# Attention and two feed-forward layers on one core: output halves issued by ScalarE, rests of the third chunk's output weights on GpSimd

## The chip, the core and the metric

The kernel runs on one core of a Trainium2 chip. Its engines each work through a queue of their own in order: TensorE (PE in the rows; PEld is its weight load), VectorE (DVE), ScalarE (ACT), GpSimd (POOL) and SyncE (SP), which here does nothing but issue DMAs. They wait for each other through semaphores. The metric is the time of one execution on the device in microseconds; the time given for a kernel is the median of its runs.

## What is computed

```python
# q, k, v: 4 batches, 8 heads, 576 rows, 64 wide; all float32
scores = scale * np.matmul(q, k.transpose(0, 1, 3, 2))
kth = np.partition(scores, -top_k, axis=-1)[..., -top_k:-top_k + 1]      # top_k = 32
scores = np.where(scores >= kth, scores, -1000000000.0)
scores = scores - np.max(scores, axis=-1, keepdims=True)
attn = np.exp(scores)
attn = attn / (np.sum(attn, axis=-1, keepdims=True) + 1e-09)
x = np.matmul(attn, v)                     # then 2304 tokens x 512
g = x @ w_gate                             # 512 -> 1536
x = (g * (1.0 / (1.0 + np.exp(-g))) * (x @ w_val)) @ w_out    # 1536 -> 512
h = x @ w_in                               # 512 -> 2048
out = (h * np.cos(h)) @ w_out2             # 2048 -> 512
```

## The kernel before

The 2304 tokens are 18 tiles of 128, taken in ten chunks (SIZES: two chunks of one tile, then eight of two). A unit is one tile and one head; there are 144. For each unit TensorE makes the scores (L598, in the first three chunks L591), ScalarE copies them to SBUF (L603), and VectorE finds the 32 largest by four rounds of max (L628) and three of striking out what was found (L631). GpSimd makes two bounds from them (L642, L646), ScalarE masks and exponentiates (L659, L670), TensorE transposes (L692), ScalarE copies (L698), TensorE multiplies by v (L745, L748), ScalarE copies that (rx, L759) and GpSimd scales it (L818, L829). VectorE has a reciprocal per group (L775) that waits for GpSimd (L777).

The first feed-forward layer runs chunk by chunk beside the attention of the chunks behind it: gate and value (L903), copies out of PSUM by ScalarE (L869, L870, L881), products by GpSimd (L957 to L959), the split of the result into a high part (ScalarE, L965) and a rest (GpSimd, L969), and the product with the output weights (L1070). From the third chunk on (c = 2, called PLAIN) float32 factors are split into a part that TensorE multiplies at full rate and a rest; each product is three such products. The second layer (L1407, L1684) follows when all chunks are through.

The output weights come in twelve tiles. For the third chunk, `wo_proc` loads a tile in float32 (L378), ScalarE makes its high part (L386), a subtraction makes the rest in place (L387), and the pair is stored (L390), so that later chunks load it ready-made (L380). Two buffers hold tiles, and a buffer comes free when TensorE has used it and the store has landed. Chunks 0 and 1 load plain weights (L376).

`y_proc` finishes a tile of the first layer's output in two halves: ScalarE copies a half out of PSUM (L1105), TensorE turns it (L1111), ScalarE copies the turned half to SBUF (L1116), and a DMA stores it (L1117) to a buffer in DRAM that the second layer loads. There is one SBUF buffer for halves, so the next half's first copy waits for the store to land. 18 tiles make 36 stores.

The order of each engine's queue is made by a planner when the program is built: every step yields an engine, a cost in microseconds, a function that emits instructions, and a due time; the planner advances a model of the engines and takes, of the steps that are ready on an engine, the one due first. A changed engine or cost of one step therefore shifts the order of everything behind it. A DMA that is emitted inside a step of another engine (as the store at L1117 inside a step of ScalarE that costs 0.27) has no cost in the model, and it stands in the queue of the engine that issues it, behind what was emitted before it. All DMAs share eight semaphores in turn, so a DMA can also have to wait for an earlier one with the same semaphore.

Of the kernel before, what the change touches and what calls it, by code (L numbers as in the profile page):

```python
# [165 lines left out]
def topk_attention_moe_moe(ctx: ExitStack, tc: tile.TileContext, qT, kT, vP, w1, wo1, w2, out):  # L166
    nc = tc.nc
# [4 lines left out]
    y1 = dram.tile([128, KT, NTOK], F32, name="y1")  # L172
# [80 lines left out]
    W1X, W1, WO = {}, {}, {}  # L253
# [52 lines left out]
    def wo_turn(c, f):  # L306
        return ev_wol.setdefault(c * NF1 + f, Event())
# [4 lines left out]
    def wo_index(c, f):  # L312
        return c * NF1 + f
# [51 lines left out]
    def wo_proc(c, f):  # L365
        k = c * NF1 + f
        yield wo_whole[f] if c <= PLAIN else wo_stored[f]
        yield r_wo.gate(wo_index(c, f))
        yield wo_turn(c, f - 1)
        due = moe_due(c, f)  # L370

        def load():
            w = moe.tile([128, 2, DM], F32R if c >= PLAIN else F32, tag="wo", name="wo", bufs=r_wo.n)
            WO[k] = w if c >= PLAIN else w[:, 0]
            if c < PLAIN:
                nc.sync.dma_start(WO[k], wo32[f])  # L376
            elif c == PLAIN:
                nc.sync.dma_start(WO[k][:, 1].bitcast(F32), wo32[f])  # L378
            else:
                nc.sync.dma_start(WO[k].bitcast(F32), wo[f])  # L380

        t = yield "DMA", 1.1 if c <= PLAIN else 1.6, load, due, True
        wo_turn(c, f).set(t - plan.LAT["DMA"], plan)
        if c == PLAIN:
            x = WO[k][:, 1].bitcast(F32)
            yield "ACT", 0.52, lambda: nc.scalar.activation(WO[k][:, 0], x, AF.Copy), due, True  # L386
            t = yield "DVE", 0.75, lambda: nc.vector.tensor_sub(WO[k][:, 1], x, WO[k][:, 0]), due, True  # L387
        ev_wo[c, f].set(t, plan)
        if c == PLAIN:
            t = yield "DMA", 2.1, lambda: nc.sync.dma_start(wo[f], WO[k].bitcast(F32)), due, True  # L390
            wo_stored[f].set(t, plan)
            r_wo.free(wo_index(c, f), t, plan)
# [461 lines left out]
    def moe_due(c, f):  # L854
        return due_unit((FIRST[c] + SIZES[c]) * H) + 20.0 + f * SIZES[c] * H * PACE / NF1
# [236 lines left out]
    def y_proc(c, i):  # L1092
        due = moe_due(c, NF1) - 80.0 * (c >= NCH - 2)
        bank = yt[i % NYB]
        y4 = bank.rearrange("p (f n) -> p f n", f=KT)
        for half in range(2):
            ko = yo_count[0]
            yo_count[0] += 1
            yield r_yo.gate(ko)
            y2 = y4[:, 2 * half:2 * half + 2]  # L1100
            st = {}

            def fetch(y2=y2):
                st["y"] = moe.tile([128, 2, 128], F32, tag="yo", name="yo", bufs=r_yo.n)
                nc.scalar.activation(st["y"], y2, AF.Copy)  # L1105

            yield "ACT", 0.27, fetch, due, True

            def turn(y2=y2):
                for j in range(2):  # L1110
                    nc.tensor.transpose(y2[:, j], st["y"][:, j], ident)  # L1111

            yield "PE", 0.22, turn, due + 2.0, True

            def store(y2=y2, half=half):
                nc.scalar.activation(st["y"], y2, AF.Copy)  # L1116
                nc.sync.dma_start(y1[:, 2 * half:2 * half + 2, i * 128:i * 128 + 128], st["y"])  # L1117

            end = yield "ACT", 0.27, store, due, True
            r_yo.free(ko, end + 2.5, plan)  # L1120
        r_y[i % NYB].free(i // NYB, end, plan)
        ev_y1[i].set(end + 2.5, plan)
# [600 lines left out]
    for c in range(NCH):  # L1723
        for f in range(NF1):
            if c:
                plan.start(wo_proc(c, f))
            if not TURNED[c]:
                plan.start(gemm_proc(c, f))
            elif f % 2:
                plan.start(turned_gemm_proc(c, f // 2))  # L1730
        plan.start(wout_proc(c))
# [52 lines left out]
```

## Time and profile before

| | |
|---|---|
| three runs, median | 1227.88 us (1226.94 to 1229.16) |
| the profiled execution | 1223.17 us |
| its span, first to last instruction | 1221.4 us |
| mean granted TensorE clock | 0.993 |
| TensorE, weight loads | 1169.9 us (96%), 1018.3 us (83%) |
| VectorE | 1002.2 us (82%) |
| ScalarE | 937.9 us (77%) |
| GpSimd | 574.8 us (47%) |
| DMA | 199.96 MB, mean 164 GB/s |

Busy shares of the whole span mix two stages: the attention with the first layer beside it, up to some 756 us, in which VectorE searches, and the rest, in which it hardly does. The rows of the section below are cut by stretch for that reason. A matmul's record reaches over the start of the next one, so a busy TensorE is not by itself one at full rate.

### The profile page before, as it was taken

The page shows a single profiled execution, that of the slowest core. Times are in us where ns is not written, and L with a number is a line of the kernel's source. Part 1 is how long each engine was busy: PE and PEld are TensorE (multiplying, and loading weights), DVE is VectorE, ACT ScalarE, POOL GpSimd, SP SyncE. Part 2 cuts the span into 40 slices and gives each one's busy share as a digit, 9 for nine tenths or more (in the row PEclk, how much of TensorE's full clock was granted, in tenths as well). Part 3 has the DMA queues.
Part 4 walks back from the last instruction along what each step waited for, and adds up shares of the span by engine and source line. Part 5 has one row for each costly group of instructions (what it writes and reads, how often), then busy time and mean ns, then how long its engine had stood idle before and what let it go on. Part 6 is the DMA issues. An engine that isn't in the chain of part 4 may idle for free. (4 is left out here: it accounts for less than half of the span.)

```text
span 1221.4 us, 23299 instructions
## 1 busy us (share of the span) xinstructions
PE 1169.9 (96%) x7720; PEld 1018.3 (83%) x7720; DVE 1002.2 (82%) x1984; ACT 937.9 (77%) x2085; POOL 574.8 (47%) x1036
## 2 busy tenths in 40 slices
PE   5799979999999999999999999999999999999998
PEld 3577646898888898898988898999999998888887
DVE  7999999999999999999999997277867778644541
ACT  4789999898889989898988887446756678755651
POOL 4898976876687876777766765300000000000000
PEclk9799999999999999999999999999999999999999
DMA  7455556665545653656545533463344276443430
GB/s 260 152 189 169 178 159 195 205 205 184 191 152 165 226 176 123 210 181 202 179 150 187 175 121 102 158 215 124 124 166 136 110 249 199 147 122 104 129 104 27
DMA packets 138985, 199.96 MB, mean 164 GB/s; under 512 B 19312, under 2 KB 88432, under 8 KB 138864
## 3 DMA queue, kind: packets, MB, share of 16 engines
q1 hardware_dynamic: 138704, 198.40, 51.1%
q8 instruction: 61, 1.00, 0.3%
q14 instruction: 60, 0.49, 0.1%
q10 hardware_dynamic: 160, 0.07, 0.0%
HBM read 152.28 MB, written 46.14 MB: 162 GB/s over the span
## 5 line engine op out<-in xcount | busy, mean ns | idle before, releaser
L628 DVE MAX8 m<-w 128x8 f32<-128x576 f32 x432 | 309.5, 747 | 1.8
L903 PE MATMUL gv<-x,w 128*128 128x256 f32 x2016 | 271.2, 286 | 0.3 <-ACT hg L870 0.3
L903 PEld LDWEIGHTS gv<-x,w 128*128 128x128 f32 x2016 | 252.2, 191 | 2.9 <-ACT hg L870 0.9
L631 DVE MATCH_REPLACE8 w<-m,w 128x576 f32<-128x576 f32 x288 | 213.0, 742 | 0.0
L1684 PE MATMUL b<-w2o,gp 128*128 128x512 f32 x864 | 202.1, 396 | 0.0
L1684 PEld LDWEIGHTS b<-w2o,gp 128*128 128x128 f32 x864 | 162.4, 188 | 38.7
L1407 PE MATMUL b<-xc,w 128*128 128x288 f32 x1344 | 182.1, 297 | 2.2 <-DVE h L1472 2.2
L1407 PEld LDWEIGHTS b<-xc,w 128*128 128x128 f32 x1344 | 180.2, 189 | 3.3 <-DVE h L1472 2.7
L1070 PE MATMUL y<-wo,gh 128*128 128x512 f32 x400 | 147.1, 414 | 4.1 <-DMA wo<-wo 1.9
L659 ACT ACTIVATE e<-s,b 128x576 f32<-128x576 f32 x144 | 113.5, 789 | 9.8 <-POOL b L642 9.5
L628 DVE MAX8 m<-s 128x8 f32<-128x576 f32 x144 | 107.2, 745 | 12.8 <-ACT s L603 11.6
L670 ACT ACTIVATE e<-e,b 128x576 f32<-128x576 f32 x144 | 114.1, 793 | 4.2 <-POOL b L646 0.3
L603 ACT ACTIVATE s<-sc 128x576 f32<-128x576 f32 x144 | 95.0, 660 | 20.3 <-PE sc L591 16.2
L698 ACT ACTIVATE pt<-tp 128x512 f32<-128x512 f32 (+1 forms) x216 | 101.4, 498 | 11.3 <-PE tp L692 10.7
L631 DVE MATCH_REPLACE8 w<-m,s 128x576 f32<-128x576 f32 x144 | 106.9, 742 | 0.0
L692 PE MATMUL tp<-ident,e 128*128 128x128 f32 x648 | 98.3, 275 | 8.8 <-ACT e L670 3.6
L1070 PEld LDWEIGHTS y<-wo,gh 128*128 128x128 f32 x400 | 75.0, 189 | 26.2 <-issue 4.0
L598 PE MATMUL sc<-K,q 128*128 128x288 f32 (+1 forms) x512 | 92.1, 307 | 3.9 <-ACT s L603 3.6
L692 PEld LDWEIGHTS tp<-ident,e 128*128 128x128 f32 x648 | 77.7, 141 | 19.7 <-ACT pt L698 5.5
L1070 PE MATMUL y<-wo,gl 128*128 128x512 f32 x208 | 84.8, 414 | 3.8 <-POOL wo L249 3.5
L598 PEld LDWEIGHTS sc<-K,q 128*128 128x128 f32 (+1 forms) x512 | 73.4, 183 | 10.8 <-ACT s L603 5.8
L748 PE MATMUL av<-pt,V 128*64 128x256 f32 (+3 forms) x832 | 75.2, 324 | 0.0
(115 smaller groups left out, 2081.6 us busy)
## 6 DMA issues: line engine op xcount, KB each, us to landing
wo<-wo SPq DMA_DIRECT2D x96, 512.0 KB, 3.6
gr<-gd SPq DMA_DIRECT2D x72, 256.0 KB, 3.2
w_raw<-in_w SPq DMA_DIRECT2D x32, 511.8 KB, 4.5
V<-in_vP SPq DMA_DIRECT2D x52, 256.0 KB, 3.0
w<-in_w SPq DMA_DIRECT2D x24, 511.5 KB, 5.7
kx<-in_kT SPq DMA_DIRECT2D x64, 144.0 KB, 3.0
wo<-wo SPq DMA_DIRECT2D x36, 256.0 KB, 3.0
gd<-h SPq DMA_DIRECT2D x32, 288.0 KB, 2.1
```

What stands on the lines that cost most here:

```text
L598: nc.tensor.matmul(sc[:r1, s, :HALF], q[:, a, (t - t0) * 128:(t - t0) * 128 + r1], k[:, s * HALF:s * HALF + HALF], start=a == 0, stop=a == 1)
L603: nc.scalar.activation(st["s"], sc[:, :, :HALF], AF.Copy)
L628: nc.vector.max(out=st["m"][:, 8 * i:8 * i + 8], in_=st["w"] if i else st["s"])
L631: nc.vector.match_replace(out=st["w"], in_to_replace=st["m"][:, 8 * i:8 * i + 8], in_values=st["w"] if i else st["s"], imm_value=LOWEST)
L659: nc.scalar.activation(st["e"], st["s"], AF.Prelu, bias=st["b"][:, 1:2], scale=SCALE, alpha=STEEP)
L670: nc.scalar.activation(st["e"], st["e"], AF.Exp, bias=st["b"][:, 2:3], scale=1.0, accum_out=smT[c, p, g][:, j:j + 1])
L692: nc.tensor.transpose(st["ps"][:, j - j0], e[:, j * 128:j * 128 + 128], ident)
L698: nc.scalar.activation(pt[:, j0:j1], st["ps"][:, :j1 - j0], AF.Copy)
L903: nc.tensor.matmul(gv[g], W1[f, kk // 2][:, a, g, kk % 2], m, start=kk == 0 and i == 0, stop=kk == KT - 1 and i == 2)
L1070: nc.tensor.matmul(bank, m, w, start=f == 0 and n == 0, stop=f == NF1 - 1 and n == len(terms) - 1)
L1407: nc.tensor.matmul(ps[b], w[:, a, side, kk], x[:, e, kk], start=start and kk == 0 and m == 0, stop=kk == 1 and m == 2, skip_group_check=True)
L1684: nc.tensor.matmul(st["o"], g[:, a, cs], W2O[f][:, b], start=f == 0 and i == 0, stop=f == NF2 - 1 and i == 2)
```

## The change

The rest of an output weight tile of the third chunk is made by GpSimd in place of VectorE, with a cost of 1.27 in the planner in place of 0.75. The store of an output half is issued by ScalarE in place of SyncE; the planner's cost of that step stays 0.27.

```diff
         if c == PLAIN:
             x = WO[k][:, 1].bitcast(F32)
             yield "ACT", 0.52, lambda: nc.scalar.activation(WO[k][:, 0], x, AF.Copy), due, True
-            t = yield "DVE", 0.75, lambda: nc.vector.tensor_sub(WO[k][:, 1], x, WO[k][:, 0]), due, True
+            t = yield "POOL", 1.27, lambda: nc.gpsimd.tensor_sub(WO[k][:, 1], x, WO[k][:, 0]), due, True
         ev_wo[c, f].set(t, plan)
...
             def store(y2=y2, half=half):
                 nc.scalar.activation(st["y"], y2, AF.Copy)
-                nc.sync.dma_start(y1[:, 2 * half:2 * half + 2, i * 128:i * 128 + 128], st["y"])
+                nc.scalar.dma_start(y1[:, 2 * half:2 * half + 2, i * 128:i * 128 + 128], st["y"])

             end = yield "ACT", 0.27, store, due, True
```

On ScalarE the first store stands behind its copy as follows; first before, then now, each instruction with the semaphores it waits for (DMAHW are those of DMAs).

```order
L295 ACTIVATE w_7_1765<-w_7_572 128x512 [waits Pool_49]
L1116 ACTIVATE yo<-y_102 128x256 [waits PE_49,Activation_49]
L698 ACTIVATE pt<-tp 128x128 [waits PE_49]
L670 ACTIVATE e,sm<-e,b_1671 128x576
L1049 ACTIVATE gh_1789<-tp 128x256 [waits PE_49]
```

```order
L295 ACTIVATE w_7_1765<-w_7_572 128x512 [waits Pool_49]
L1116 ACTIVATE yo<-y_102 128x256 [waits PE_49,Activation_49]
L1117 DMA y_63<-yo 128x2x128 [waits DMAHW0_49,Activation_49]
L698 ACTIVATE pt<-tp 128x128 [waits PE_49]
L670 ACTIVATE e,sm<-e,b_1671 128x576
L1049 ACTIVATE gh_1789<-tp 128x256 [waits PE_49]
```

The store waits for ScalarE's own semaphore and, in 25 of the 36 cases, for that of an earlier DMA; the copy pt and all behind it now stand behind the store.

On SyncE the same two first stores go, and the loads of the second chunk's output weights (L376) and of keys (kx) move up; one piece of the difference.

```order
 L338 DMA wo_65<-wo 128x512
 L515 DMA qx<-in_qT 64x2x256 x2
-L1117 DMA y_63<-yo 128x2x128
 L376 DMA wo<-wo_65 128x512 x3
-L1117 DMA y_63<-yo 128x2x128
 L490 DMA kx<-in_kT 64x576 x2
 L376 DMA wo<-wo_65 128x512 x3
```

Both stores leave the queue and nothing else moves in these rows.

On GpSimd the first subtraction stands where the third chunk's first layer begins; b are the bounds of a unit, x, th and vv parts of the layer, K a split key. Before:

```order
L818 TENSOR_TENSOR rs<-rx,rs 128x256
L642 TENSOR_TENSOR b_2146<-m,cst 128x2
L646 TENSOR_TENSOR b_2146<-b_2146 128x1
L829 TENSOR_TENSOR x<-rs,x 128x256
L642 TENSOR_TENSOR b_2222<-m,cst 128x2
L501 TENSOR_TENSOR K<-kx,K 64x576
L646 TENSOR_TENSOR b_2222<-b_2222 128x1
L957 TENSOR_SCALAR th<-th 128x256
```

and now:

```order
L818 TENSOR_TENSOR rs<-rx,rs 128x256
L642 TENSOR_TENSOR b_2146<-m,cst 128x2
L387 TENSOR_TENSOR wo<-wo 128x512
L829 TENSOR_TENSOR x<-rs,x 128x256
L646 TENSOR_TENSOR b_2146<-b_2146 128x1
L642 TENSOR_TENSOR b_2218<-m,cst 128x2
L646 TENSOR_TENSOR b_2218<-b_2218 128x1
L501 TENSOR_TENSOR K<-kx,K 64x576
L957 TENSOR_SCALAR th<-th 128x256
```

The subtraction and the product x stand between the two halves of one unit's bounds. From here on all engines' orders differ in small moves up to the end of the attention; the kinds and numbers of matmuls are the same.

## Rows read from the trace of the kernel before

**Rows 1.** Stretches: length, busy us of PE, PEld, DVE, ACT, POOL (instructions).

```profile
0.00:200.00 200.00, 165.35 (x819) 115.05 (x820) 184.72 (x387) 164.70 (x362) 157.94 (x266) 0.96 0.58 185
...
200.00:756.00 556.00, 545.55 (x4155) 491.87 (x4154) 543.88 (x1123) 490.98 (x1192) 402.07 (x745) 1.00 0.55 175
...
204.00:285.00 81.00, 79.77 (x635) 72.18 (x634) 79.92 (x163) 73.29 (x176) 63.66 (x110) 1.00 0.66 212
...
780.00:860.00 80.00, 79.55 (x573) 75.94 (x572) 54.52 (x106) 42.72 (x93) 0.00 (x0) 1.00 0.57 187
...
1020.00:1215.00 195.00, 195.00 (x837) 157.29 (x836) 95.09 (x142) 115.27 (x195) 0.00 (x0) 1.00 0.38 114
```

**Rows 2.** Timeline of PE, one run in each stage: start us, us, what.

```profile
287.85 3.11 PE L903 MATMUL gv<-x,w 128*128 128x256 f32 x24
...
781.57 3.60 PE L903 MATMUL gvl<-x,w 128*128 128x256 f32 x28
```

**Rows 3.** PE's waits, 200 to 780 us: who waits for whom: us, times, longest.

```profile
PE y L1111 <- ACT yo L1105: 2.5, 5, 0.9
PE sc L598 <- ACT s L603: 2.1, 3, 1.3
PE tp L692 <- ACT rx L759: 1.6, 1, 1.6
PE y L1070 <- DMA wo<-wo: 1.2, 2, 0.7
...
PE y L1070 <- POOL gl L969: 0.2, 1, 0.2
```

**Rows 4.** L387 as a group (busy, mean ns); L299 alike: ns least, median, most.

```profile
L387 DVE TENSOR_TENSOR wo<-wo 128x512 fp32r<-128x512 f32 x12 | 10.0, 831 | 0.4 <-ACT wo L386 0.4
...
L299 POOL TENSOR_TENSOR w<-w,w x12: 1265/1276/1288, 113.7 to 186.6; 128x512 fp32r<-128x512 f32 x12
L299 DVE TENSOR_TENSOR w<-w,w x12: 669/690/1523, 115.9 to 188.9; 128x512 fp32r<-128x512 f32 x12
```

**Rows 5.** Timeline of POOL and DVE around one subtraction.

```profile
244.00 0.73 POOL L818 TENSOR_TENSOR rs<-rx,rs 128x256 f32<-128x256 f32 x1
...
244.06 1.22 DVE L387 TENSOR_TENSOR wo<-wo 128x512 fp32r<-128x512 f32 x1
245.20 0.08 DVE L631 MATCH_VALUE_LOAD w<-m,w 128x8 f32 x1
```

**Rows 6.** DVE's waits, 200 to 760 us.

```profile
DVE sm L775 <- POOL sm L777: 3.8, 4, 1.7
DVE m L628 <- ACT s L603: 3.5, 6, 1.3
```

**Rows 7.** Issues of L1117 and of ScalarE's only DMAs: ns least, median, most.

```profile
L1117 SPq DMA_DIRECT2D y<-yo x36: 360/371/663, 166.3 to 853.7; - x36
...
L465 ACTq DMA_DIRECT2D qr<-in_qT x2: 547/627/707, 0.9 to 1.5; - x2
```

**Rows 8.** SyncE's wait at the stores; the stores' size and median us to landing.

```profile
SPq L1117 <- ACT yo L1116: 56.8, 20, 5.5
...
y<-yo SPq DMA_DIRECT2D x36, 128.0 KB, 1.9
```

**Rows 9.** Timeline of SP and PE behind the first store.

```profile
166.75 5.10 SPq L376 DMA_DIRECT2D wo<-wo  x3
...
169.47 2.03 PE L1070 MATMUL y<-wo,xw 128*128 128x512 f32 x2 [2.33 <-DMA wo<-wo]
```

**Rows 10.** Timeline of ACT, SP and PE at the store of 206.69 us.

```profile
206.69 0.38 ACT L1116 ACTIVATE yo<-y 128x256 f32<-128x256 f32 x1
206.95 0.65 ACT L603 ACTIVATE s<-sc 128x576 f32<-128x576 f32 x1
...
207.09 0.37 SPq L1117 DMA_DIRECT2D y<-yo  x1
...
209.80 0.40 ACT L870 ACTIVATE hg<-gv 128x256 f32<-128x256 f32 x1
...
210.25 1.70 PE L903 MATMUL gv<-x,w 128*128 128x256 f32 x12
```

**Rows 11.** Timeline of ACT at the store of 288.44 us; idle before in brackets.

```profile
288.44 0.36 ACT L1116 ACTIVATE yo<-y 128x256 f32<-128x256 f32 x1
...
290.88 0.78 ACT L659 ACTIVATE e<-s,b 128x576 f32<-128x576 f32 x1 [0.66 <-POOL b L642]
```

## The prediction

> **What bounds the kernel now.** I read the table of stretches first. From 200 to 756 us, the bulk of the attention with the first feed-forward layer beside it, VectorE is busy 543.88 of 556.00 us and TensorE 545.55 [rows 1]: both look full. ScalarE has 556.00 - 490.98 = 65.0 us without work, one part in nine, and GpSimd more. After 756 us VectorE is no longer full (54.52 of 80.00 us from 780 to 860) while TensorE is (79.55 of 80.00) [rows 1]. So the question is whether the time from 200 us on is set by VectorE, which this change relieves, or by TensorE, which it doesn't.
>
> A busy TensorE need not be a full one, since a matmul's record reaches over the start of the next. So I compare spacing: 24 matmuls of L903 inside the attention take 3.11 us, and 28 of the same form in the last chunk, after all attention, 3.60 us [rows 2]. Taking off one record's tail of about 0.29 us, that is 2.82/23 = 0.123 and 3.31/27 = 0.123 us from start to start. TensorE does not run any looser beside the attention than where nothing but matmuls is left. What it loses shows in its list of waits: ten groups, 10.2 us together from 200 to 780, nearly all ended by ScalarE, and by GpSimd 0.2 us [rows 3]. My reading: from 200 us to the end TensorE's work sets the time, and an edit counts by what it does to these ten microseconds. VectorE's full row is a second, nearly equal bound.
>
> The Trainium skill (Perfetto Trace Analysis, Identifying the Most-Contended Engine) says that matmul busy time is a poor measure and that the share of weight loading should be used. By it TensorE is 491.87/556.00 = 88% full and VectorE 98%, and relieving VectorE would pay. The trace agrees about the busy row, but the share has no 100% here: between 1020 and 1215 us, where TensorE is busy without a break, weight loading is 157.29/195.00 = 81% [rows 1]. By the rule the sum would be the first rival's below.
>
> **Part 1: rests of the third chunk's output weights, VectorE to GpSimd.** VectorE loses 12 subtractions of 831 ns mean, 10.0 us busy [rows 4]; a record overlaps the next by 0.08 us (the one at 244.06 lasts 1.22, the next row starts at 245.20 [rows 5]), so 12 x 0.75 = 9.0 us of its queue go. If VectorE alone set the time, that is -9.0. With TensorE as the bound only those of its waits can go that hang on the attention's progress: scores waiting for the copy out of PSUM, 2.1 us, and transposes waiting for the copy rx, 1.6 us [rows 3], 3.7 us at most. They end at ScalarE, not at VectorE, and VectorE's own waits are 3.8 us for GpSimd and 3.5 for ScalarE [rows 6], so not all of it can go. Between 0 and -9.0 I take **-2.0**.
>
> GpSimd gains 12 subtractions. It does the same form at L299 in 1.276 us median [rows 4]: 12 x 1.276 = 15.3 us, in the stretch where VectorE now does them (204 to 285 us). GpSimd is busy 63.66 of 81.00 us there [rows 1], so 17.3 us idle hold 15.3, with nothing to spare. Behind each subtraction in its queue stand the bounds of the softmax (L642, L646), the gate products and the rests of gh that TensorE multiplies; in the new order the first one stands between the two halves of one unit's bounds. Each weight tile is ready later too: 1.276 - 0.831 = 0.45 us, plus up to one GpSimd operation ahead of it (0.73 us, L818 [rows 5]). All twelve passed on would be 12 x 1.2 = +14 us; none, 0. TensorE now waits for GpSimd 0.2 us in 580 [rows 3], the planner's cost for the moved step (1.27) is the measured one, and it places the matmuls behind it accordingly. I take **+1.0**, near the low end.
>
> One row speaks for the move: at 244.06 the subtraction on VectorE takes 1.22 us instead of the 0.69 median of its like at L299, while GpSimd's L818 started at 244.00 [rows 4, 5]. The Trainium skill (SBUF — State Buffer, Who interferes with whom) says why: a VectorE instruction with two SBUF inputs contends with a GpSimd instruction that reads SBUF, and the second to issue waits. After the change VectorE has only one-input searches there, and by this rule GpSimd would also get some time back; without it the charge stays at 15.3 us. The sum goes by the rows alone.
>
> **Part 2: 36 stores from SyncE's queue to ScalarE's.** SyncE loses 36 issues of 0.371 us [rows 7] and the waits in front of them, 56.8 us in 20 cases [rows 8]; what stood behind can leave earlier. Most had no reader in a hurry: the wait of TensorE on weight loads is 1.2 us from 200 on [rows 3]. The 2.33 us at 169.47, where the load stands right behind a store at 166.75 [rows 9], lies before 200 us, where TensorE is busy only 165.35 of 200.00 us [rows 1] and the attention decides when the third chunk starts. Bounds 0 and -3.5; I take **-0.5**. The moment of the store itself hardly changes, since SyncE already stands waiting when ScalarE is done (L1116 ends 206.69 + 0.38 = 207.07, issue 207.09 [rows 10]).
>
> ScalarE pays. Its store has to wait for the end of the copy before it (the program makes it wait for ScalarE's own semaphore), and the queue behind it waits for the issue. Today the next operation starts 0.12 us before the copy's end (206.95 against 207.07 [rows 10]). After: 0.03 us to the issue, 0.37 us issue, and the overlap lost, 0.52 us a store; 36 x 0.52 = 18.7 us. The only DMAs that ScalarE issues today took 0.627 us median, another shape [rows 7], which would make it 0.78. The planner still charges 0.27 for copy and store, so it moves nothing out of the way. Two stores lie before 200 us, eight after 780, where ScalarE is busy only 42.72 of 80.00 us [rows 1] and which I cost at nothing (the idle half covers them; uncovered they are 8 x 0.52 = 4.2 us). The 26 between: 13.5 us if all of it reached TensorE, 0 if ScalarE's idle time took it all. I followed each of the 26 in the timeline from the copy to the next idle time that makes up 0.52 us, asking whether TensorE meanwhile started on an output of ScalarE with less than that to spare. In 15 it did. The one at 206.69 is such a case: no idle time before the copy hg at 209.80, which ends at 210.20, and L903 starts at 210.25, so 0.47 us reach it [rows 10]. In 11 not: after 288.44 comes 0.66 us of idle time at 290.88 before anything of TensorE is touched [rows 11]. The 15 shortfalls add to 5.5 us; where two follow closely, the first also gives the second some slack. I take **+4.5**.
>
> A DMA also waits for a semaphore of an earlier DMA in 25 of the 36 stores, which on ScalarE would hold more than the store. I cost it at nothing: SyncE has issued all that stands ahead of such a store and then waits for ScalarE, 56.8/20 = 2.8 us on average, longer than the 1.9 us in which such a store lands [rows 8]. If that cover goes, each of the 25 can hold ScalarE for up to 1.9 us.
>
> **Sum.** -2.0 + 1.0 - 0.5 + 4.5 = +3.0 us. The profiled execution took 1223.17 us (span 1221.4 and 1.8 around it), 0.4% under the median of the three runs, 1227.88. Profiled: 1226.2; as a median: **1230.9**.
>
> **Rivals.** *VectorE sets the time* (faster). It is 98% busy and from 204 to 285 us it has 81.00 - 79.92 = 1.1 us idle [rows 1]; if every matmul run hangs on attention results, the 9.0 us go through, 1218.9, and if half go through and ScalarE's gaps fill, about 1224. Against it stands the equal spacing of matmuls [rows 2]. It decides if TensorE's idle time in 200 to 756 falls well under its present 10.4 us. *The gaps vanish in ScalarE's idle time* (no change): 65 us of idle time take 13.5, VectorE's relief and GpSimd's load cancel, and the end stays near 1228. For it: only 15 of 26 stores meet a tight reader at all. *GpSimd comes late* (slower): 15.3 us into 17.3 us idle delays weights and bounds, TensorE waits 0.8 us at each of 12 tiles, 9.6 us in place of the 1.0: 1227.88 + 3.0 + 8.6 = 1239.5. It decides once the wait for a rest is longer than the matmuls that the planner has put ahead of it. Against: the planner counts the move at its measured price.
>
> **Chances.** Forecast (ScalarE's gaps reach TensorE, +1.5 to +8) 0.40; no change 0.34; VectorE decides 0.17; GpSimd late 0.09. Range 1224 to 1236: it holds the first two and the weaker half of VectorE's case, and leaves out 0.09 below and 0.09 above. Changes under 0.2%, 2.5 us, can't be told from none here. Slower by more: 0.46; within: 0.37; faster: 0.17.
>
> **What would show it.** Right: ScalarE's next operation after L1116 starts about 0.4 us after its end; TensorE's waits ended by ScalarE grow from under 9 us to about 13 between 200 and 780; VectorE has 5 to 10 us idle more in the attention, and its last search ends earlier than 756 by less than 9 us. GpSimd is 75 to 79 us busy from 204 to 285. Wrong: TensorE's idle time shrinks and the end moves by what VectorE saved; or TensorE's waits on GpSimd and weights grow by microseconds; or the stores' wait for a DMA semaphore shows as a ScalarE gap of over a microsecond.

## The result, and the profile after

The changed kernel takes 1242.05 us in the median of six runs (1238.74 to 1246.35), the kernel before 1228.24: a ratio of 1.0111, with an interval of 1.0090 to 1.0131, or 13.6 us (11.1 to 16.1) more. The forecast was +3.0, and its range ended at 1236. Single executions of one kernel lie mostly within 3 us of its median, a few as far as 7. The first profiled execution of the kernel before (1223.17 us) lies 5 us under its median, and that of the changed kernel (1246.35 us) is the slowest of its six, 4.3 us over its own. So the two traces lie 23 us apart where the kernels lie 13.6, and a difference between them is evidence only if it is larger than what a second execution of the kernel before, of 1230.06 us, shows against the first; it is called the second execution of before. In what follows a ratio of 0.1% is 1.23 us.

The stretches of the changed kernel that answer to [rows 1], in the same columns, and one short stretch behind the attention:

```profile
200.00:756.00 556.00, 540.42 (x4073) 482.78 (x4072) 530.98 (x1090) 482.22 (x1170) 407.22 (x746) 1.00 0.55 173
204.00:285.00 81.00, 78.00 (x622) 70.28 (x622) 76.73 (x161) 74.04 (x177) 70.05 (x119) 1.00 0.61 199
780.00:860.00 80.00, 74.20 (x499) 67.84 (x499) 37.37 (x75) 31.28 (x74) 7.26 (x11) 0.96 0.51 160
800.00:810.00 10.00, 8.88 (x53) 8.88 (x54) 2.81 (x7) 3.05 (x9) 0.00 (x0) 0.66 0.29 87
```

VectorE is 12.9 us less busy from 200 to 756 than before and TensorE 5.1, with 82 matmuls fewer in the same time; against the second execution of before (538.46 and 543.01 us, 4109 matmuls) it is 7.5 us, 2.6 us and 36 matmuls. Either way VectorE was relieved and TensorE got less done. The loudest row is the third. From 780 to 860 us TensorE runs 499 matmuls where it ran 573 [rows 1]. That is where the prediction charged nothing. Part of the difference is only lag, since this execution comes to 780 us with some 12 us of work behind; the table further below takes that out.

The waits of TensorE from 200 to 780 us, as in [rows 3], and below them those of VectorE from 200 to 760, as in [rows 6]:

```profile
PE y L1111 <- ACT yo L1105: 4.1, 7, 2.7
PE gv L903 <- ACT hg L870: 3.6, 5, 1.3
PE sc L598 <- ACT s L603: 2.0, 5, 0.7
...
PE y L1070 <- POOL gl L969: 0.3, 1, 0.3
```

```profile
DVE m L628 <- ACT s L603: 12.5, 14, 2.0
DVE sm L775 <- POOL sm L777: 6.9, 6, 2.5
```

ScalarE is what both wait for most. TensorE waits for the copy of an output half (L1105) 4.1 us in place of 2.5 (2.0 in the second execution of before), once 2.7 us long, and VectorE waits for ScalarE's copies 12.5 us in place of 3.5 (6.2 in the second). TensorE waits for GpSimd as little as before.

Why is L1105 late? Two views of the store say it: its issues with the time from issue to landing, and the idle time of ScalarE in front of L1105 (us, times).

```profile
L1117 ACTq DMA_DIRECT2D y<-yo x36: 366/366/417, 167.3 to 874.9; - x36
...
DMA to landing us min/median/max: 1.8/2.7/6.4
```

```profile
  DMA y<-yo: 10.7, 8
```

Before, the store landed in 1.9 us in the median and 3.8 at most, and ScalarE waited 5.2 us in six places for it. Now it is 2.7 in the median and 6.4 at most, and 10.7 us in eight places. That sum alone doesn't tell what a kernel loses: with the stores still on SyncE it is 8.4 us with the rests moved and 10.3 with a planner's number changed, two kernels that come further below. The longest wait, in the timeline of ScalarE (idle time before in brackets):

```profile
793.81 0.38 ACT L1116 ACTIVATE yo<-y 128x256 f32<-128x256 f32 x1 [2.02 <-PE y L1111]
794.22 0.37 ACTq L1117 DMA_DIRECT2D y<-yo  x1
794.63 0.38 ACT L978 ACTIVATE th<-gvl 128x256 f32<-128x256 f32 x1 [0.44 <-ACT yo L1116]
796.11 0.42 ACT L965 ACTIVATE gh<-vv 128x256 fp32r<-128x256 f32 x1 [1.09 <-DVE vv L943]
800.69 0.38 ACT L1105 ACTIVATE yo<-y 128x256 f32<-128x256 f32 x1 [4.16 <-DMA y<-yo]
```

Both costs of the store stand in five rows: the hole of 0.44 us behind the copy (at least that behind all 36 copies), and then 4.16 us in which ScalarE, with one buffer for halves, stands waiting for a store that takes 6.45 us to land. SyncE's timeline at that time, of the changed kernel and then of the kernel before at the same place, tells why:

```profile
790.62 0.43 SPq L1332 DMA_DIRECT2D xr<-y  x1
791.10 0.94 SPq L1247 DMA_DIRECT2D wr<-w2d  x2
792.13 0.38 SPq L380 DMA_DIRECT2D wo<-wo  x1
792.55 0.43 SPq L1332 DMA_DIRECT2D xr<-y  x1
793.03 1.22 SPq L1247 DMA_DIRECT2D wr<-w2d  x2
794.74 0.37 SPq L1332 DMA_DIRECT2D xr<-y  x1
```

```profile
791.38 5.65 SPq L1117 DMA_DIRECT2D y<-yo  x2
798.27 0.33 SPq L380 DMA_DIRECT2D wo<-wo  x1
```

Before, SyncE sent one store at 791.38, stood waiting for the copy of the next, sent that at 796.66, and no load in between. Now it doesn't wait, and it has sent loads of 128 to 512 KB all the way; by the times of issue and landing in the trace, 1600 KB had been issued and not landed when the store was issued at 794.22. The Trainium skill (DMA: Bandwidth & Descriptors, Issuing engines are not separate DMA queues) says that DMAs of all issuing engines run on the same 16 DMA engines and interleave, so that a second issuer saves only issue time. These rows agree: ScalarE's own queue did not get the store past SyncE's loads. The amount under way alone does not set the landing, though: at 719.91 us of the same trace a store with 640 KB ahead of it landed in 1.83 us.

The chain of work that ended last runs through it, which makes it a loss of the whole execution:

```profile
794.22 6.45 DMA y<-yo
...
801.12 0.69 PE y L1111 x2
801.81 6.60 PE gvl L903 x36
...
809.14 3.25 DMA y<-yo
...
828.28 6.39 DMA wo<-wo
```

The second landing in it, 3.25 us at 809.14, had no load ahead of it; why it took so long is open.

The wait may have cost once more in this execution. TensorE stood 3.11 us until 801.12, its granted clock from 800 to 810 us was 0.66, between the levels of 1.2 and 2.4 GHz, and 36 matmuls of L903 took 6.95 us from 801.46. Before, 24 of them took 3.11 [rows 2], so 36 would take some 4.6, and just ahead of the wait 36 took 4.55.

### The profile page after: what moved, and what is told of

It is laid out like the page before. It is cut to its first block, busy times and chain, and to the rows that moved or that the text cites. A ratio compares the mean times of both kernels' runs of the same rounds, so it can differ in the third digit from the quotient of the medians.

```text
span 1244.6 us, 23225 instructions
## 1 busy us (share of the span) xinstructions
PE 1181.2 (95%) x7720; PEld 1023.1 (82%) x7720; DVE 1000.0 (80%) x1972; ACT 938.2 (75%) x2085; POOL 584.7 (47%) x1048
## 3 DMA queue, kind: packets, MB, share of 16 engines
q10 hardware_dynamic: 9952, 4.79, 1.3%
## 5 line engine op out<-in xcount | busy, mean ns | idle before, releaser
L903 PE MATMUL gv<-x,w 128*128 128x256 f32 x2016 | 272.9, 287 | 3.6 <-ACT hg L870 3.6
L903 PEld LDWEIGHTS gv<-x,w 128*128 128x128 f32 x2016 | 252.8, 191 | 7.8 <-ACT hg L870 5.2
L670 ACT ACTIVATE e<-e,b 128x576 f32<-128x576 f32 x144 | 112.9, 784 | 4.4 <-POOL th L958 0.5
L603 ACT ACTIVATE s<-sc 128x576 f32<-128x576 f32 x144 | 94.1, 654 | 19.5 <-PE sc L591 16.1
L969 POOL TENSOR_TENSOR gl<-vv,gh 128x256 fp32r<-128x256 f32 x84 | 62.0, 738 | 44.2 <-ACT gh L965 30.3
```

The source lines that it names most:

```text
L603: nc.scalar.activation(st["s"], sc[:, :, :HALF], AF.Copy)
L670: nc.scalar.activation(st["e"], st["e"], AF.Exp, bias=st["b"][:, 2:3], scale=1.0, accum_out=smT[c, p, g][:, j:j + 1])
L903: nc.tensor.matmul(gv[g], W1[f, kk // 2][:, a, g, kk % 2], m, start=kk == 0 and i == 0, stop=kk == KT - 1 and i == 2)
```

## The experiments

**The store alone, and the hold given back.** Theory A: SyncE's wait for the copy had kept the loads back, and the late landing costs. Theory B: the hole in ScalarE's queue costs. Theory C: the rests on GpSimd cost. Theory D: the planner's new order costs. In the edits below `y1[...]` stands for the slice of y1 in full.

```diff
-                nc.sync.dma_start(y1[:, 2 * half:2 * half + 2, i * 128:i * 128 + 128], st["y"])
+                nc.scalar.dma_start(y1[:, 2 * half:2 * half + 2, i * 128:i * 128 + 128], st["y"])
```

> Only the store goes to ScalarE's queue; the rests stay on VectorE, and the planner's order is that of the kernel before on every engine. Theory A (late landing): while SyncE stood waiting for the copy it sent no loads, so the store found the DMA engines nearly empty; now loads run on, the store lands later (2.7 us median in the changed kernel against 1.9), and since there is one yo buffer the next L1105, and all of ScalarE behind it, waits. Then this kernel carries most of the +13.8 us: 1235 to 1242 us, landing median 2.4 us or more, ScalarE's waits for the landing of y 9 us or more (5.2 before). Theory B (the 0.44 us hole behind each copy alone, the one that the prediction priced at +4.5): 1230 to 1234 us, landings as before. Theory C (the rests on GpSimd cost it) and theory D (the new order costs it): under 1231 us.

Measured: 1239.81 us against 1229.58, ratio 1.0092 (1.0064 to 1.0119). Most of the loss comes with the store, and no other instruction had to change place for it. The landing median is 2.0 us and ScalarE's waits for landings are 8.4 us in six places, both less than A asked for, but single stores take 6.4 and 4.1 us.

The hold is given back by a DMA of 4 bytes:

```diff
                 nc.scalar.dma_start(y1[:, 2 * half:2 * half + 2, i * 128:i * 128 + 128], st["y"])
+                nc.sync.dma_start(dram.tile([1, 1], F32, name=f"z{i}_{half}"), st["y"][:1, 0, :1])
```

> As the kernel with only the store moved, and SyncE also sends a 4-byte DMA out of the yo buffer at the place where it sent the store, so that SyncE again stands waiting until the copy is done. Theory A (late landing for want of that hold): landing median back to 1.8 to 2.1 us, ScalarE's waits for y's landing back to 4 to 7 us, and the time falls by 5 us or more against the kernel with only the store moved, to 1229 to 1234 us. Theory B (the hole alone): the same time as that kernel, within 2 us.

1237.42 us, ratio 1.0070 (1.0047 to 1.0094): 2.4 us less than with the store alone, where A wanted 5; the slowest of its six runs (1239.33) lies just under the fastest of the five with the store alone (1239.34). ScalarE's waits in front of L1105 are back where they were before:

```profile
  DMA y<-yo: 5.1, 5
```

What it did is plain in the timelines of SyncE and of ScalarE at the place of the long wait:

```profile
792.10 0.93 SPq L1248 DMA_DIRECT2D wr<-w2d  x2
795.22 0.24 SPq L1118 DMA_DIRECT2D z<-yo  x1
```

```profile
795.23 0.37 ACTq L1117 DMA_DIRECT2D y<-yo  x1
...
797.43 0.37 ACT L1105 ACTIVATE yo<-y 128x256 f32<-128x256 f32 x1
```

SyncE stands from 793.03 to 795.22, the next L1105 starts 2.20 us after the store's issue and waits for nothing. So A's mechanism is real, but with the waits for landings repaired 8.6 us of the 11.3 stay: the larger share is B's.

**The hole.** The kernel before, its store on SyncE, and 4 bytes on ScalarE as well:

```diff
                 nc.sync.dma_start(y1[:, 2 * half:2 * half + 2, i * 128:i * 128 + 128], st["y"])
+                nc.scalar.dma_start(dram.tile([1, 1], F32, name=f"z{i}_{half}"), st["y"][:1, 0, :1])
```

> The kernel before, with the store of 128 KB still on SyncE (which so still stands waiting for the copy), and on ScalarE behind it an added DMA of 4 bytes out of the yo buffer. ScalarE gets the hole of the store and nothing else changes. Theory B (the hole itself is what costs, since ScalarE's idle time doesn't take it up): close to the kernel with only the store moved and SyncE held, ratio 1.005 to 1.009, 1235 to 1240 us, with 0.3 to 0.45 us idle after L1116. Theory A (late landing alone): 1228 to 1231 us. The prediction's own price of the hole, +4.5 us of a possible 13.5, gives 1232 to 1235 us.

1233.16 us, ratio 1.0045 (1.0028 to 1.0063), or 5.5 us (3.4 to 7.7), with a hole of 0.29 us, between what B and A asked for and at the prediction's own price. With the lost overlap of 0.12 us, 0.41 us a store cost 5.5 here and 0.56 us a store 8.6 in the kernel with SyncE held. Both kernels carry 36 added DMAs of 4 bytes, whose own cost no run shows. The next one keeps the store on ScalarE and puts it behind the compute instruction that follows the copy:

```diff
+    late = ()
+    def do(self, engine, fn):
+        late, self.late = (self.late, ()) if engine == "ACT" else ((), self.late)
+        for f in (fn, *late):
+            f()
...
-            fn()
+            self.do(engine, fn)
...
-                nc.sync.dma_start(y1[:, 2 * half:2 * half + 2, i * 128:i * 128 + 128], st["y"])
+                plan.late = (lambda y=st["y"]: nc.scalar.dma_start(y1[...], y),)
```

> As the kernel with only the store moved, but ScalarE's queue has the store one instruction later: behind the compute instruction that follows the copy L1116. By then the copy is done or nearly, so ScalarE need not run empty for the store. Theory B: if the hole comes from waiting for the copy's end, the idle time after L1116 goes and, with the store issued while ScalarE still computes, the time falls to 1229 to 1234 us; if it comes from the 0.37 us of issue, which would stand between two instructions wherever it is, nothing changes and the time stays at 1238 to 1241. Theory A: 1236 to 1240 us in either case, since the loads run ahead as they do there.

1232.14 us, ratio 1.0024 (1.0009 to 1.0040). Behind the copy the hole is gone in 33 of 36 cases, as its ScalarE timeline shows beside that of the kernel with the 4 bytes above it:

```profile
289.98 0.37 ACT L1116 ACTIVATE yo<-y 128x256 f32<-128x256 f32 x1
290.38 0.22 ACTq L1118 DMA_DIRECT2D z<-yo  x1
290.64 0.78 ACT L670 ACTIVATE e<-e,b 128x576 f32<-128x576 f32 x1 [0.29 <-ACT yo L1116]
```

```profile
289.36 0.37 ACT L1116 ACTIVATE yo<-y 128x256 f32<-128x256 f32 x1
289.62 0.77 ACT L670 ACTIVATE e<-e,b 128x576 f32<-128x576 f32 x1
289.75 0.37 ACTq L1117 DMA_DIRECT2D y<-yo  x1
```

L670 starts 0.11 us before the copy ends, and the store is issued while it runs. Where the next instruction is short, a part of the hole comes back behind it:

```profile
382.38 0.47 ACT L1116 ACTIVATE yo<-y 128x256 f32<-128x256 f32 x1
382.64 0.37 ACT L698 ACTIVATE pt<-tp 128x128 f32<-128x128 f32 x1
382.88 0.37 ACTq L1117 DMA_DIRECT2D y<-yo  x1
383.29 0.78 ACT L670 ACTIVATE e<-e,b 128x576 f32<-128x576 f32 x1 [0.28 <-ACT pt L698]
```

That is so in 13 cases, behind instructions of 0.28 to 0.44 us, with 0.14 to 0.33 us of idle time. Between the kernel with the store alone and this one lie 0.68%, 8 us, for nothing but one place in the queue. That is B: most of the hole was the wait for the copy, and the 0.37 us of issue show only where a short instruction doesn't cover them. The long landing after the attention is still there (issue at 787.22, the next L1105 at 793.84 after 4.79 us of idle time), and still the kernel is at 1232, where A asked for 1236 to 1240: late landings without the hole cost 2.9 us (1.1 to 4.9).

**The last eight stores.** Only those of the two chunks after the attention:

```diff
-                nc.sync.dma_start(y1[...], st["y"])
+                (nc.scalar if i >= 14 else nc.sync).dma_start(y1[...], st["y"])
```

> The kernel before, with the last eight of the 36 stores (the two chunks after the attention) on ScalarE's queue and the other 28 on SyncE's. In the kernels with all stores on ScalarE, the one at 787 to 794 us lands after 6.4 to 6.6 us, with 1600 KB of loads ahead of it, and the stretch from 780 to 840 us takes 5 to 6 us longer than in the kernel before. Theory A (late landing): these eight stores alone cost 4 to 6 us, 1232.5 to 1235 us, ratio 1.0035 to 1.005, with a landing over 5 us and ScalarE's wait for it of 3 to 5 us. Theory B (the hole alone): 8 x 0.44 = 3.5 us at most, where ScalarE is half idle: 1228 to 1230 us, as the prediction put it.

1234.25 us, ratio 1.0058 (1.0040 to 1.0076): 7.1 us (4.9 to 9.3) for eight of 36 stores, more than A asked for and twice what B allowed at most. Here the long landing is 4.88 us, with 1600 KB ahead of it again, and ScalarE waits 2.57 and 2.26 us behind the first two, less than A asked for. The reverse edit on the changed kernel:

```diff
-                nc.scalar.dma_start(y1[...], st["y"])
+                (nc.scalar if i < 14 else nc.sync).dma_start(y1[...], st["y"])
```

> The changed kernel with those last eight stores put back on SyncE. Theory A: 4 to 7 us faster than the changed kernel, 1235 to 1238 us, and the clock of TensorE stays at 1.00 from 790 to 820 us. Theory B: 1240 to 1242 us.

1238.53 us, ratio 1.0100 (1.0081 to 1.0118). In the medians 3.5 us less than the changed kernel, but the ratios, each against the kernel before on its chip, differ by 0.1% only. That is less than expected, and the interval of either reaches twice that to each side. So what the last eight cost when they are moved alone does not come back here when they are put back. The clock stays at 1.00, as expected. The trace shows the effect where it should be. The table takes the matmuls that the first execution of before does between 200 and 780 us and between 780 and 900, and gives how many microseconds longer each kernel's execution took for the same share of its matmuls (weighted by their usual spacing):

| kernel | 200 to 780 | 780 to 900 |
|---|---|---|
| before, second execution | 6.1 | 0.9 |
| hole of 4 bytes only | 5.8 | 1.2 |
| store only, SyncE held | 13.9 | 1.7 |
| store only | 9.8 | 6.4 |
| store one instruction later | 6.0 | 6.3 |
| last eight stores only | 7.4 | 3.8 |
| changed | 11.0 | 9.3 |
| changed, last eight back on SyncE | 15.0 | 1.3 |
| rests only | 4.3 | 3.1 |
| new order, rests on VectorE (below) | 11.6 | 2.8 |
| first 28 one instruction later, last eight on SyncE (below) | 4.9 | 0.7 |
| changed, stores one instruction later (below) | 11.2 | 4.5 |

The left column has the spread of single executions in it (6.1 us between two of the same kernel). The right one separates them: 0.7 to 3.1 wherever SyncE waits in front of the last stores, 3.8 to 9.3 where loads run ahead of them. The 3.1 and 2.8 belong to the planner's new order with the stores on SyncE; in the kernel with the rests only, 1.7 us of it are one wait of TensorE for a load of weights. Each row is one execution, and in the medians the difference is smaller, as the last two kernels of this section show.

**The rests and the order.**

```diff
-            t = yield "DVE", 0.75, lambda: nc.vector.tensor_sub(WO[k][:, 1], x, WO[k][:, 0]), due, True
+            t = yield "POOL", 1.27, lambda: nc.gpsimd.tensor_sub(WO[k][:, 1], x, WO[k][:, 0]), due, True
```

> Only the twelve rests go to GpSimd, with the planner's new order; the store stays on SyncE. Theory A and theory B: within 3 us of the kernel before, 1225 to 1231 us (the prediction's own terms for this part were -2.0 and +1.0). Theory C (GpSimd late) and theory D (the new order): 1234 us or more. VectorE's queue is 9 to 10 us shorter in all of them.

1233.26 us, ratio 1.0033 (1.0016 to 1.0050), 4.1 us more. VectorE's 9 us bought nothing: in this kernel too it waits for ScalarE instead, 12.0 us from 200 to 760, where the two executions of before have 3.5 and 6.2:

```profile
DVE m L628 <- ACT s L603: 12.0, 13, 2.0
```

Three kernels take it apart. The first keeps the new order and leaves the work on VectorE, the second keeps the old order and does the work on GpSimd, the third only tells the planner another number:

```diff
-            t = yield "DVE", 0.75, lambda: nc.vector.tensor_sub(WO[k][:, 1], x, WO[k][:, 0]), due, True
+            t = yield "POOL", 1.27, lambda: nc.vector.tensor_sub(WO[k][:, 1], x, WO[k][:, 0]), due, True
```

> The planner is told that the rests are on GpSimd, so every engine gets the changed kernel's order, but they run on VectorE (in the place in VectorE's queue that falls out of the program's order) and the store stays on SyncE. Theory D (the order itself): the same time as the kernel with only the rests moved, and away from 1228 us if that one is. Theory C (GpSimd's 15 us): back at 1228 within 3 us. If the kernel with only the rests moved is at 1228 too, this one says whether an order made for other costs is worth anything: VectorE then has 9 us that the planner doesn't know of, up to +9 if VectorE sets the time.

```diff
-            t = yield "DVE", 0.75, lambda: nc.vector.tensor_sub(WO[k][:, 1], x, WO[k][:, 0]), due, True
+            t = yield "DVE", 0.75, lambda: nc.gpsimd.tensor_sub(WO[k][:, 1], x, WO[k][:, 0]), due, True
```

> The twelve rests run on GpSimd, but the planner is still told that they are 0.75 us on VectorE, so every other engine keeps the order of the kernel before; stores on SyncE. If the +3.7 us of the kernel with only the rests moved come from the planner's new order (theory D), this one is at or under the kernel before: 1224 to 1230 us. If they come from GpSimd's extra 15 us (theory C), it is at 1233 us or more, since GpSimd's time is now not planned for. The prediction's rival of VectorE as the bound would show here best: VectorE loses 9 us and nothing else is rearranged, 1219 to 1225 us.

```diff
-            t = yield "DVE", 0.75, lambda: nc.vector.tensor_sub(WO[k][:, 1], x, WO[k][:, 0]), due, True
+            t = yield "DVE", 0.85, lambda: nc.vector.tensor_sub(WO[k][:, 1], x, WO[k][:, 0]), due, True
```

> The kernel before with one number changed: the planner is told 0.85 us for a rest on VectorE, not 0.75. Nothing is moved between engines, but every engine's order changes from about 200 us on. It says how much a new order costs by itself. Theory D (the order before happened to be a good one, and a new one costs some microseconds): 1231 us or more, as with the rests on GpSimd (1233). Theory C (it is GpSimd's extra work): within 2 us of the kernel before.

The new order with the work on VectorE: 1236.87 us, 1.0068 (1.0045 to 1.0091); VectorE has 9 us there that the planner doesn't know of, so this is not the price of the order alone. The old order with the work on GpSimd: 1231.31 us, 1.0025 (1.0010 to 1.0040), so VectorE's relief is no gain there either. That is 3.1 us (1.2 to 4.9) with the old order, between what C (1233 or more) and D (1230 at most) asked for, and GpSimd does show in it. VectorE waits for GpSimd's step in front of its reciprocal 15.4 us, where the two executions of before have 3.8 and 5.5 and the kernel with the rests only has 1.9:

```profile
DVE sm L775 <- POOL sm L777: 15.4, 11, 4.0
```

The number alone: 1.0059 (1.0033 to 1.0084). The same with 0.65 in place of 0.85:

> The kernel before with the planner told 0.65 us for a rest on VectorE, not 0.75 (the other way than 0.85, which cost 0.6%). Theory D, any new order costs some microseconds because the order before is a good one among many: 1231 us or more again. Against it: within 2 us of the kernel before, if only the order with the dearer rest is a bad one.

1.0043 (1.0027 to 1.0059). So a planner's number that is 0.1 us higher or lower, with no work moved, costs 0.4 to 0.6%, as much as the moved rests. An order alone is enough to cost the 0.33%, and GpSimd's work in the old order costs nearly as much, so the four kernels don't split the 0.33% between the two. Within the new order the move even gains: 1.0068 on VectorE, 1.0033 on GpSimd.

The second profile of the kernel before, for comparison:

> The kernel before, profiled once more: its first profiled execution was 5 us under its median. All theories: 1227 to 1231 us. It shows where those 5 us lie, and so which of the waits named for the changed kernels are also there in an ordinary execution of the kernel before.

It took 1230.06 us. Its ScalarE waits 5.4 us in five places for the landing of y, so the 5.2 of the first one was no accident.

**Both causes out.** The store one instruction later for the first 28, the last eight on SyncE, with the rests on VectorE:

```diff
+                if i < 14:
+                    plan.late = (lambda y=st["y"]: nc.scalar.dma_start(y1[...], y),)
+                else:
+                    nc.sync.dma_start(y1[...], st["y"])
```

> The rests on VectorE as before; the first 28 stores on ScalarE's queue, one instruction later than the copy, and the last eight on SyncE. Both causes together: the deferred store took the hole away (1232.1 us with all 36 so) and the late landing at the end cost 4 to 6 us of that. Theories A and B together: 1225 to 1228 us, at or a little under the kernel before. If it stays at 1231 or more, the late landings in the attention cost too, or something else that the store on ScalarE brings.

1229.98 us, ratio 1.0020 (1.0005 to 1.0035). Expected was at or under the kernel before; it isn't, and by the ratios it gains only 0.04% on the deferred store with all 36. The same edits on the changed kernel, and the changed kernel with all stores deferred:

> The changed kernel, rests on GpSimd, with both causes of the store part taken out: the first 28 stores on ScalarE's queue one instruction behind the copy (no hole), the last eight on SyncE (no late landing after the attention). If hole and late landing are all that the store costs, what is left is the price of the moved rests: 1231 to 1234 us, as with the rests moved alone (ratio 1.0033), 8 to 11 us under the changed kernel. If the store's price lies elsewhere too (late landings inside the attention, as the 5.5 us one at 295 us), 1236 us or more.

> The changed kernel with all 36 stores one instruction behind the copy, so without the hole and with the late landings. By the price of the hole alone (5.5 us) 1236 to 1238 us; by what the deferred store saved with the rests on VectorE (8 us) 1233 to 1236 us. The difference to the kernel with the last eight stores also on SyncE, on the same chip, is the price of the late landings after the attention: 3 to 6 us by the traces, under 2 us if the two kernels with the rests on VectorE (1.0024 and 1.0020) tell it rightly.

Deferred: 1238.43 us, 1.0082 (1.0062 to 1.0101). Deferred and the last eight on SyncE: 1235.94 us, 1.0062 (1.0046 to 1.0079). The deferral takes 3.6 us off in the medians, less than either price of the hole asked for, and its interval overlaps that of the changed kernel; ScalarE's waits for landings are 15.1 us in eleven places there. SyncE for the last eight takes 2.5 more, between the 2 that the two kernels with the rests on VectorE allowed and the 3 to 6 of the traces. Hole and tail together took 6.1 us of 13.8 off in the medians, and what is left is not the 0.33% of the rests but 0.62%. One place of the rest can be named, in the timelines of ScalarE and TensorE (the store's line is L1118 here):

```profile
295.19 0.43 ACTq L1118 DMA_DIRECT2D y<-yo  x1
...
300.51 0.38 ACT L1105 ACTIVATE yo<-y 128x256 f32<-128x256 f32 x1 [2.68 <-DMA y<-yo]
```

```profile
300.94 0.44 PE L1111 MATMUL y<-ident,yo 128*128 128x128 f32 x2 [2.44 <-ACT yo L1105]
```

It is a late landing again, this time inside the attention, with 800 KB of loads ahead of it in the changed kernel, which has it too (issue 295.31, landing 5.54 us, 2.74 us of ScalarE, 2.68 of TensorE). Not all of it is the move: with the store on SyncE ScalarE waits 1.79 us at this place in the second execution of before and 1.83 in the kernel with the rests only. No version here beats the kernel before.

## Why the prediction was wrong, point by point

*What bounds the kernel.* Right in the main: TensorE sets the time, its waits end at ScalarE, and relieving VectorE moved nothing forward. The waits ended by ScalarE grew from 8.8 to 13.1 us between 200 and 780, the 13 that was named, but 10.0 stand already in the second execution of before, and landings and the new order are in the 13.1 beside the hole. The rival of VectorE as the bound falls, since both kernels with VectorE relieved and the store left alone are slower. By the Trainium skill's rule on weight loading (Perfetto Trace Analysis, Identifying the Most-Contended Engine) they would have gained; the runs go against it.

*Part 1, -2.0 and +1.0.* Measured +4.1 (2.0 to 6.1). The step that failed is "it places the matmuls behind it accordingly": the prediction took the planner's new order as good as the old one. It had no term for an order, and two kernels that change nothing but an order cost 5 to 7 us. GpSimd did what was priced, at 1.29 us an operation, and it is 70.05 us busy from 204 to 285, under the 75 to 79 named; TensorE waits no longer for it in the new order (0.3 us), so the rival of GpSimd coming late, which hangs on TensorE's waits, gets no support. In the old order the moved work comes with 3.1 us all the same, and with VectorE's waits for GpSimd about three times as long; that these cause it is not shown, and how much of the 4.1 is order and how much is work stays open.

*Part 2, the hole, +4.5.* Right in mechanism, too low in size, and this is the larger part of what the store costs. A store takes 0.44 us of idle time and the lost overlap of 0.12, 0.56 against the 0.52 of the sum; that much was right. What reached the end was not: a smaller hole alone measured +5.5 us, the full one with SyncE held +8.6 (5.8 to 11.5), and the deferral took off 8. The step that failed is the count of how much ScalarE's idle time takes up: 5.5 us by following 26 stores to the next idle time, cut to 4.5, and nothing for the last eight. Which of the stores cost more than was followed, no run shows.

*Part 2, SyncE's relief, -0.5, bounds 0 and -3.5.* The sign was wrong: the late landings that came with it cost 2.9 us (1.1 to 4.9) without the hole, and 2.4 us come off when the hold is given back. The prediction asked what stood behind SyncE's wait and could now leave earlier, and never what leaving earlier does to the store. The wait was also a hold on the loads. The front of this document says that the next half's first copy waits for the store to land, and no term of the sum carried it; the 1.9 us to land went in as a constant.

*Part 2, the eight stores after 780 us, at nothing.* "The idle half covers them" failed: ScalarE's idle time there is in front of L1105, on the chain that ends last, and these eight, moved alone, cost 7.1 us (4.9 to 9.3) where 4.2 was named as the most. Putting them back on SyncE gave less in all three kernels where it was done: 0.04, 0.11 and 0.20% by the ratios. Why moving and putting back differ is open.

*The DMA semaphores, at nothing.* Right for ScalarE: in all 36 cases the issue comes 0.03 us after the copy. It came back on SyncE: one of its loads now waits 4.5 us for a store of ScalarE's.

*The sum.* For the store alone the measured terms add up: 8.6 for the hole with SyncE held and 2.9 for the landings without the hole make 11.5, and 11.3 were measured. With 4.1 for rests and order that is 15.6, inside the 11.1 to 16.1 of the changed kernel and 2.0 over its 13.6. So no single step carries the miss: the sum had +4.5, -0.5 and -1.0 for the three. That the hole taken out of the changed kernel gave back only 3.6 shows that they do not simply add there. How much the late landings inside the attention cost alone, and why the order before is better than three others, stays open. A second buffer for halves, which would take away the wait for the landing, was not tried.

## What to carry to other kernels

A queue that stands waiting in front of a store also holds back the loads behind it. Before a store is moved to another queue, ask what the freed queue will send, and which buffer waits for the store to land. If a busy engine has to issue a DMA on its own result, place it behind that engine's next instruction, if that one is long enough to cover the issue. And where a planner sets the order, price a new order from a kernel that changes only a number, before a gain of half a per cent is put down to the work that was moved.

## What the runs showed of the hardware

- A store of 128 KB from ScalarE's queue landed in 1.8 us in most cases with no load under way (at 470.52 in the changed kernel), in 2.8 and 3.3 in two of them (644.37 and 809.14), and in 4.9 to 6.6 with 1600 KB of loads of SyncE's queue ahead of it, in five kernels.
- A DMA that ScalarE issues on the result of its own last instruction left 0.44 us or more without work in all 36 cases; issued one instruction later, at the same 0.37 us of issue, it left no more than the kernel before has behind instructions of 0.6 us and more, and 0.14 to 0.33 us behind 13 of 0.28 to 0.44 us.
- A wait of 3.11 us of TensorE was followed by a granted clock of 0.66 over 10 us in the changed kernel; in the kernel with only the store moved, a wait of 3.1 us was not (1.00 from 790 to 820 us). What tells the two apart is open.
